# First chunk of an attention and feed-forward kernel: two transfers issued sooner, five additions and the rest of U and V issued later, products with low weight parts issued last

## The chip, the cores and the metric

The kernel runs on one core of a Trainium2 chip. The metric is the device time of one execution in microseconds (us). Engines are named as the profile names them: PE (TensorE matmuls) and PEld (its weight loads), DVE (VectorE), ACT (ScalarE), POOL (GpSimd), and SP, whose queue issues every DMA of this kernel. Each engine works through its own list of instructions in order; they meet only at semaphores.

## The reference

The computation is windowed attention followed by a low-rank token mix and a feed-forward layer, all on float32 inputs:

```python
scores = scale * np.matmul(q, k.transpose(0, 1, 3, 2))     # 8 batches, 8 heads, 576 tokens, 64 wide
mask_plain = (rel >= 0) & (rel < 32)                       # heads 0 to 3
mask_dil = (rel >= 0) & (rel < 128) & (rel % 4 == 0)       # heads 4 to 7
attn = softmax(where(mask, scores, -1e9));  x = (attn @ v), heads side by side: 576 x 512 per batch
h = x.transpose(0, 2, 1) @ U @ V                           # U 576 x 32, V 32 x 576: mixes tokens
u = x + h.transpose(0, 2, 1)
ch = np.maximum(u @ w_ch1, 0.0) @ w_ch2                    # 512 -> 2048 -> 512
return u + ch
```

U, V and the two weights arrive as 64-bit floats, viewed as pairs of 32-bit words.

## The kernel before

**Chunks.** The 36 token tiles of 128 rows are processed by the feed-forward layer in chunks: chunk 0 holds tiles 0 to 3, chunk 1 tiles 4 and 5, every later chunk three tiles. A chunk goes through the 16 slices f of the hidden dimension: `layer1(f)` makes `ph` (12 matmuls of 512 columns in chunk 0), ACT and DVE turn it into a high part `hh` and a low part `hl`, and `layer2(f-1)` adds to one accumulator per tile (4 tiles x 3 matmuls in chunk 0). Each product is made of three, because operands are split into a high and a low part: high x high, high x low weight, low x high weight. In chunk 0 the `ph` buffer of one slice is free again when DVE has made the slice's `hl`, since the fourth accumulator takes one of the two buffers.

**Weights.** All weights are fetched and split during chunk 0. Pieces are numbered in the order of their use: first U (piece 0), V (piece 1), the rest of U and V ("uv", piece 2), then w1 and w2 slices in turn. A piece is fetched into one of four `raw` buffers (`fetch64`, SP), rescaled (`narrow_hi` and `narrow_lo`, lines 199 and 203, ACT), put together (`narrow_b`, lines 207 and 209; 209 runs on DVE for w1 pieces and on POOL for w2 pieces and uv), and split (`narrow_c`: high part of w1 on ACT, line 213, of w2 on DVE, line 215; low part `w1l` or `w2l` on POOL, line 216). Line 209 is the last reader of the raw buffer. `weight_step` runs twice per slice f, moves four pieces one stage on each, and fetches one more: the fetch waits on SP until line 209 of an earlier piece has freed its raw buffer, and everything behind it on SP waits too.

**Attention beside it.** Batch 0's attention (groups 0 to 8, two query blocks of 64 each) is done before chunk 0 in `first_batch`. Batch 1's groups 9 to 17 are spread over chunk 0. Step s of `attention_steps(1)` issues, on SP, v of group 9+s-1 (two DMAs, `load_v`, line 353), k of group 9+s+2 (line 332), and the rows of an earlier group that are scattered into x (`spread_rows`, line 518, five or six DMAs); on PE it issues pv of group 9+s-2 (line 475), the scores s of group 9+s (line 418) and the transposes ptp (line 452); DVE places pv, takes the row minimum and copies the transposed pt (line 458). So v of a group is issued one step ahead of its use. Four v buffers hold two groups.

**The mix of batch 0.** The upper half of the columns of batch 0's x lies in the dilated order of the tokens in `xps`. `leave` writes it to DRAM in eight DMAs (line 823), `come` reads it back in token order in five (line 828). The mixes add h to x: line 595 is one matmul of 256 columns, line 597 the addition by DVE, ten of each. Only the sum u + ch at the end of the chunk and the transposes for chunk 1 (tile 4) read the result; the transposed u that chunk 0 multiplies was made in `first_batch` by `mix_turned`.

**What sets the order.** Inside chunk 0 the order on every engine is the order of the program (`manual_schedule`). Beside the matmuls the program calls `slot()`: two slots inside layer 1, one behind it, three inside layer 2, one behind that, seven for each slice. A list `queue` of pairs (position, work) is taken in order of position; slot number n stands at position 0.01223 n, so one slice f is 0.0856 and chunk 0 ends at 1.33. Batch 1's step s stands at 0.012 + 0.075 s. From chunk 1 on, a planner sets the order of the instructions.

Of the kernel before, what the change touches and what calls it, by code (L numbers as in the profile page):

```python
# [10 lines left out]
F32 = mybir.dt.float32  # L11
F32R = mybir.dt.float32r
# [13 lines left out]
P = 128  # L26
# [105 lines left out]
def batch_parts(b):  # L132
    parts = []
    tok = 0
    while tok < S:
        t, row = divmod(b * S + tok, P)
        n = min(P - row, S - tok)
        parts.append((t, row, n, tok))
        tok += n
    return parts  # L140
# [3 lines left out]
def attention_moe_kernel(ctx: ExitStack, tc: tile.TileContext, qk0, qk2, vv, masks, wide, ident, ut, vt, uv, w1, w2, out):  # L144
# [122 lines left out]
    def narrowed(i):  # L267
        narrow_first(i)
        narrow_second(i)
# [35 lines left out]
    def send(to):  # L305
        while NSMALL + len(sent) < to:
            n = NSMALL + len(sent)
            sent[n] = True
            pipe[n] = fetch64(n)
# [9 lines left out]
    def x_tile(t):  # L319
        if t not in xt:  # L320
            xt[t] = xpool.tile([P, DM], F32, tag="x", name=f"x{t}")
        return xt[t]
# [258 lines left out]
    def t_evict(b, c):  # L581
        r = [slice(i * RANK, (i + 1) * RANK) for i in range(4)]
        tp = t_ps.pop((b, c))
        t_sb[b, c] = ts_ = ts0[c]
        nc.scalar.copy(out=ts_[r[0]], in_=tp[r[0]])
        nc.scalar.copy(out=ts_[r[3]], in_=tp[r[0]])
        nc.vector.tensor_tensor(out=ts_[r[1]], in0=tp[r[0]], in1=ts_[r[0]].bitcast(F32), op=ALU.subtract)

    def mix(b, i, c):
        assert 1 in finished  # L590
        t, row, n, tok = batch_parts(b)[i]
        rs = slice(row, row + n)
        mp = psum.tile([P, HALF_D], F32, tag="ps", name=f"m{b}_{i}_{c}")
        o = 64 + tok - row
        nc.tensor.matmul(mp, lhsT=vs[:, o:o + P], rhs=t_sb[b, c], start=True, stop=True)
        x = x_tile(t)[rs, c * HALF_D:(c + 1) * HALF_D]
        nc.vector.tensor_tensor(out=x, in0=x, in1=mp[rs], op=ALU.add)

    u_ps = {}

# [244 lines left out]
    early_open = ExitStack()  # L845
    early = early_open.enter_context(tc.tile_pool(name="early", bufs=1))
    u32 = early.tile([P, NU * RANK], F32, name="u32")
    ts0 = [early.tile([P, HALF_D], F32R, name=f"ts0_{c}") for c in range(2)]
    q_sb = early.tile([P, NQ, UNITS, 2, QB], F32, name="q_sb")
    idle_sb = early.tile([P, DM], BF16, name="idle_sb")  # L850
    nc.vector.memset(idle_sb, 0.0)
# [2 lines left out]
    for i in range(2):  # L854
        for q1 in q1_sb:
            nc.vector.memset(q1[i * QB:(i + 1) * QB, :, 1 - i], 0.0)
    for t in ts0 + [ts_sb]:
        nc.gpsimd.memset(t[2 * RANK:3 * RANK].bitcast(F32), 0.0)
    for t in pts:
        nc.gpsimd.memset(t, 0.0)  # L860
# [11 lines left out]
    for g in range(1, NGB):  # L872
# [6 lines left out]
        if g == U_AT:  # L879
            pipe[0] = fetch64(0)  # L880
    load_v(NGB - 1, 0)
    for i in range(3, 6):
        send(NSMALL + i)
        if i < 5:
            load_q(NGB + i - 3)
    first_batch()

    held = {}
# [16 lines left out]

    n0 = len(batch_parts(0))
    queue = [(AHEAD_AT[0], lambda: ahead(0)), (AHEAD_AT[1], lambda: ahead(1))]
    queue += [(0.15 + 0.01 * p, lambda p=p: leave(p)) for p in range(NDP)]
    queue += [(0.22 + 0.005 * i, lambda i=i: come(i)) for i in range(n0)]
    queue += [(0.18 + 0.012 * i, lambda i=i: mix(0, i, 0)) for i in range(n0)]  # L910
    queue += [(0.27 + 0.008 * i, lambda i=i: mix(0, i, 1)) for i in range(n0)]

    def fetch_rest():
        pipe[2] = fetch64(2)
# [1 line left out]
    def split_first_u():  # L916
        finish_u(u32[:, 0:4 * RANK], slice(0, 4))
        finish_u(u32[:, 4 * RANK:5 * RANK], slice(8, 9))

    queue += [(0.04, fetch_rest), (0.10, lambda: narrowed(2)), (0.12, lambda: add_low(2, nc.gpsimd)),  # L920
              (0.14, lambda: finish(2)), (0.17, split_first_u)]
    for b in range(1, B):
        lo, hi = (1.5 * b - 2 - LO0, 1.5 * b - 0.5) if b > 2 else (LO2, HI2 + MARGIN)
        its = batch_items(b)
# [11 lines left out]
    for c, tiles in enumerate(CHUNKS):  # L936
        slots = [0]
        nt = len(tiles)
        uh, ul = (e[:, :, 0:nt * P] for e in uts.pop(c))
        acc = [psum.tile([P, DM], F32, tag="acc" if i < CT else "ph", name=f"acc{c}_{i}", bufs=3 if i < CT else 2)  # L940
               for i in range(nt)]
        ht = {}

        def slot():
            pos = (tiles[0] + nt * slots[0] / ((nt + 3) * FC - 3)) / CT
            slots[0] += 1
            while queue and queue[0][0] <= pos:
                queue.pop(0)[1]()

        def layer1(f):  # L950
            assert place_of[f, 0] in finished
            ph = psum.tile([P, CTOK], F32, tag="ph", name=f"ph{c}_{f}", bufs=2)[:, 0:nt * P]
            w1h, w1l = held_w[f][0:2]
            ks = (2, 3, 0, 1) if c == f == 0 else range(KC)
            seq = [(w, u, k) for w, u in ((w1h, uh), (w1l, uh), (w1h, ul)) for k in ks]
            for n, (w, u, k) in enumerate(seq):
                nc.tensor.matmul(ph, lhsT=w[:, k, :], rhs=u[:, k, :], start=(n == 0), stop=(n == len(seq) - 1))  # L957
                if n % KC == KC - 1 and n < len(seq) - 1:
                    slot()
            hh = work.tile([P, CTOK], F32R, tag="hh", name=f"hh{c}_{f}", bufs=2)[:, 0:nt * P]  # L960
            hl = work.tile([P, CTOK], F32R, tag="hl", name=f"hl{c}_{f}", bufs=2)[:, 0:nt * P]
            nc.scalar.activation(out=hh, in_=ph, func=AF.Relu)  # L962
            nc.vector.scalar_tensor_tensor(out=hl, in0=ph, scalar=0.0, in1=hh.bitcast(F32),  # L963
                                           op0=ALU.max, op1=ALU.subtract)
            ht[f] = (hh, hl)

        def layer2(f):
            assert place_of[f, 1] in finished
            hh, hl = ht.pop(f)
            w2h, w2l = held_w[f][2:4]  # L970
            for i in range(nt):
                ss = slice(i * P, (i + 1) * P)
                for n, (h, w) in enumerate(((hh, w2h), (hh, w2l), (hl, w2h))):
                    nc.tensor.matmul(acc[i], lhsT=h[:, ss], rhs=w,  # L974
                                     start=(f == 0 and n == 0), stop=(f == FC - 1 and n == 2))
                if f < FC - 1 and i < nt - 1:
                    slot()

        more = list(CHUNKS[c + 1]) if c + 1 < NCHUNK else []
        for f in range(FC):  # L980
            if c == 0 and f == F_MID - 1:
                after_first()
            if c == 0:
                weight_step()
            layer1(f)
            if f < FC - 1:
                slot()
            else:
                for t in more[0:2]:
                    transp(t)  # L990
            if c == 0:
                weight_step()
            if f > 0:
                layer2(f - 1)
                if f < FC - 1:
                    slot()
        for t in more[2:]:
            transp(t)
        layer2(FC - 1)
        if c == 0:  # L1000
            order.__exit__(None, None, None)
        for i, t in enumerate(tiles):
            x = xt.pop(t)
            nc.vector.tensor_tensor(out=x, in0=acc[i], in1=x, op=ALU.add)  # L1004
            nc.sync.dma_start(out=out[t * P:(t + 1) * P, :], in_=x)
# [87 lines left out]
```

## Time and profile before

| | |
|---|---|
| time, median of 3 runs | 980.51 us (979.42 to 981.93) |
| profiled execution, its own time | 979.55 us |
| its span, first to last instruction | 977.8 us |
| granted TensorE clock, mean | 0.996 |
| busy: PE / DVE / ACT / POOL | 965.0 / 576.5 / 355.9 / 282.8 us |
| chunk 0 (first matmul of layer 1 to the last of layer 2) | 34.9 to 158.9 us of the span |

In a timeline a row gives start, duration, engine, line, operation, the tiles as out<-in, the shapes, the count, and in brackets the idle time before it with what ended it. Engine SPq is SP issuing a DMA; the duration is that of the issue, not of the transfer. In a row of a window the figures are busy us of each engine with the number of instructions, then the granted clock and the share of DMA engines that were busy. Matmul durations overlap: the pace is read from the distance of starts.

### The profile page before, as it was taken

The page shows a single profiled execution, that of the slowest core. Times are in us where ns is not written, and L with a number is a line of the kernel's source. Part 1 is how long each engine was busy: PE and PEld are TensorE (multiplying, and loading weights), DVE is VectorE, ACT ScalarE, POOL GpSimd, SP SyncE. Part 2 cuts the span into 40 slices and gives each one's busy share as a digit, 9 for nine tenths or more (in the row PEclk, how much of TensorE's full clock was granted, in tenths as well). Part 3 has the DMA queues.
Part 4 walks back from the last instruction along what each step waited for, and adds up shares of the span by engine and source line. Part 5 has one row for each costly group of instructions (what it writes and reads, how often), then busy time and mean ns, then how long its engine had stood idle before and what let it go on. Part 6 is the DMA issues. An engine that isn't in the chain of part 4 may idle for free.

```text
span 977.8 us, 17663 instructions
## 1 busy us (share of the span) xinstructions
PE 965.0 (99%) x5906; PEld 835.0 (85%) x5906; DVE 576.5 (59%) x1935; ACT 355.9 (36%) x861; POOL 282.8 (29%) x490
## 2 busy tenths in 40 slices
PE   9989999999999999999999999999999999999998
PEld 7677878988988888888988889888898888999997
DVE  5677777784677747665467746767446864211211
ACT  6755664352344314343244423334233421111110
POOL 4665566252233304241133402343022410000000
PEclk9989999999999999999999999999999999999999
DMA  9477654442344325442233414533323502200000
GB/s 336 142 242 237 196 166 126 132 141 77 89 118 142 97 51 146 125 117 84 76 103 114 130 35 118 148 101 106 89 61 105 158 24 60 81 1 1 33 1 33
DMA packets 100331, 106.14 MB, mean 109 GB/s; under 512 B 12496, under 2 KB 85392, under 8 KB 100240
## 3 DMA queue, kind: packets, MB, share of 16 engines
q1 hardware_dynamic: 100240, 105.01, 36.3%
q8 instruction: 48, 0.79, 0.4%
q14 instruction: 43, 0.35, 0.1%
HBM read 82.94 MB, written 17.89 MB: 103 GB/s over the span
## 4 chain that ended last, share of the span: by engine, by line
PE 89%; DMA 2%; DVE 2%; POOL 2%; issue 2%; SPq 1%; ACT 1%; DVEq 0%; POOLq 0%; ACTq 0%
PE acc L974 38%; PE ph L957 38%; PE pv L475 4%; PE s L405 3%; PE s L418 2%; PE t L555 1%; SPq L518 1%; DMA qkr<-qk 1%; DMA x<-spare 1%; PE ptp L452 1%; PE m L577 1%; POOL v L209 1%; PE idle_ps L867 1%; POOL w1l L216 1%; DVE pt L464 0%
## 5 line engine op out<-in xcount | busy, mean ns | idle before, releaser
L974 PE MATMUL acc<-w2h,hh 128*128 128x512 f32 x576 | 228.4, 397 | 1.1 <-DVE x L1004 0.8
L974 PE MATMUL acc<-w2l,hh 128*128 128x512 f32 x576 | 228.1, 396 | 0.9 <-POOL w2l L216 0.9
L382 POOL TENSOR_TENSOR qks<-qkr,qks 128x160 fp32r<-128x160 f32 x192 | 103.4, 538 | 429.8 <-issue 209.0
L963 DVE SCALAR_TENSOR_TENSOR hl<-ph,hh 128x384 fp32r<-128x384 f32 (+2 forms) x192 | 106.3, 554 | 180.0 <-ACT hh L962 179.1
L974 PE MATMUL acc<-w2h,hl 128*128 128x512 f32 x576 | 212.5, 395 | 0.0
L962 ACT ACTIVATE hh<-ph 128x384 fp32r<-128x384 f32 (+2 forms) x192 | 93.3, 486 | 288.5 <-PE ph L957 279.2
L957 PE MATMUL ph<-utl,w1h 128*128 128x384 f32 (+2 forms) x768 | 171.7, 338 | 0.0
L957 PE MATMUL ph<-uth,w1h 128*128 128x384 f32 (+2 forms) x768 | 170.9, 339 | 0.5 <-DVE hl L963 0.5
L957 PE MATMUL ph<-uth,w1l 128*128 128x384 f32 (+2 forms) x768 | 170.2, 338 | 0.0
L441 ACT ACTIVATE p<-p,nmax 128x160 f32<-128x160 f32 (+1 forms) x288 | 109.3, 406 | 133.4 <-DVE nmax L437 132.2
L957 PEld LDWEIGHTS ph<-uth,w1h 128*128 128x128 f32 x768 | 136.9, 188 | 18.7 <-DVE hl L963 1.4
L464 DVE STREAM_TRANSPOSE pt<-p 32x128 f32<-32x128 f32 x432 | 130.2, 301 | 22.6 <-ACT p L441 17.1
L957 PEld LDWEIGHTS ph<-utl,w1h 128*128 128x128 f32 x768 | 134.2, 188 | 4.5 <-issue 0.8
L957 PEld LDWEIGHTS ph<-uth,w1l 128*128 128x128 f32 x768 | 133.4, 188 | 4.7 <-issue 1.2
L974 PEld LDWEIGHTS acc<-w2h,hl 128*128 128x128 f32 x576 | 108.0, 188 | 23.9 <-issue 1.2
L381 ACT CAST qks<-qkr 128x288 fp32r<-128x288 f32 x192 | 80.8, 430 | 127.9 <-PE s L405 63.4
L974 PEld LDWEIGHTS acc<-w2h,hh 128*128 128x128 f32 x576 | 108.5, 188 | 19.9 <-issue 1.2
L974 PEld LDWEIGHTS acc<-w2l,hh 128*128 128x128 f32 x576 | 108.5, 188 | 17.7 <-POOL w2l L216 1.5
L385 POOL TENSOR_TENSOR qks<-qkr,qks 64x128 fp32r<-64x128 f32 x192 | 90.0, 469 | 15.0
L434 DVE TENSOR_TENSOR p<-s,wide_sb 128x160 f32<-128x160 f32 x192 | 59.3, 319 | 50.2 <-PE s L405 48.1
L437 DVE CUSTOM_DVE_ANT_0 p<-s,p 128x160 f32<-128x160 f32 x192 | 59.7, 320 | 3.5
L475 PEld LDWEIGHTS pv<-v,pt 96*64 96x64 f32 x1152 | 41.1, 138 | 23.5 <-issue 13.0
(90 smaller groups left out, 765.9 us busy)
## 6 DMA issues: line engine op xcount, KB each, us to landing
qkr<-qk SPq DMA_DIRECT2D x192, 144.0 KB, 2.2
v<-vv SPq DMA_DIRECT2D x126, 130.0 KB, 2.4
raw<-w SPq DMA_DIRECT2D x25, 512.0 KB, 4.1
out<-x SPq DMA_DIRECT2D x36, 256.0 KB, 2.4
zd<-z SPq DMA_DIRECT2D x120, 64.0 KB, 2.1
xt<-zd SPq DMA_DIRECT2D x30, 256.0 KB, 2.9
k<-qk SPq DMA_DIRECT2D x18, 320.0 KB, 5.1
raw<-w SPq DMA_DIRECT2D x14, 256.0 KB, 3.4
```

What stands on the lines that cost most here:

```text
L381: nc.scalar.copy(out=t[:, 0:QK2], in_=raw)
L382: nc.gpsimd.tensor_tensor(out=t[:, QK2:], in0=raw[:, P:], in1=t[:, P:QK2].bitcast(F32), op=ALU.subtract)
L385: eng.tensor_tensor(out=t[lo, 0:P], in0=raw[lo, 0:P], in1=t[lo, 0:P].bitcast(F32), op=ALU.subtract)
L434: nc.vector.tensor_tensor(out=p_sb[:, u, :], in0=sp[:, 0:KW], in1=held[0][:, kind], op=ALU.add)
L437: nc.vector.tensor_tensor_reduce(out=p_sb[rs, u, 0:w], in0=a, in1=c, scale=-1.0 / 8.0, scalar=3.0e38, op0=ALU.add, op1=ALU.min, accum_out= ...
L441: nc.scalar.activation(out=p_sb[:, u, 0:w], in_=p_sb[:, u, 0:w], func=AF.Exp, bias=nmax[:, u:u + 1], scale=-1.0,)
L464: nc.vector.transpose(out=pt[WIN * k:WIN * (k + 1), :, rs], in_=p_sb[rs, :, o:o + WIN])
L475: nc.tensor.matmul(pv[rs, u, :], lhsT=pt[:, u, rs], rhs=loaded[g, 1, i][0:KB, u, :], start=True, stop=True)
L957: nc.tensor.matmul(ph, lhsT=w[:, k, :], rhs=u[:, k, :], start=(n == 0), stop=(n == len(seq) - 1))
L962: nc.scalar.activation(out=hh, in_=ph, func=AF.Relu)
L963: nc.vector.scalar_tensor_tensor(out=hl, in0=ph, scalar=0.0, in1=hh.bitcast(F32), op0=ALU.max, op1=ALU.subtract)
L974: nc.tensor.matmul(acc[i], lhsT=h[:, ss], rhs=w, start=(f == 0 and n == 0), stop=(f == FC - 1 and n == 2))
```

## The change

Five things change, all in chunk 0 or ahead of it.

1. v of groups 9 and 10 (four DMAs) is issued ahead of `first_batch`, behind the first two weight pieces and ahead of k of groups 9 and 10; each of these k moves ahead of the weight piece that it followed. Steps 1 and 2 of batch 1 then issue no v.
2. `leave` moves from positions 0.15 to 0.19 to 0.24 to 0.28, `come` from 0.22 to 0.24 to 0.44 to 0.50.
3. The ten mixes of 256 columns at 0.18 to 0.30 become five of 512 columns (`mix_rest`, lines 577 and 579) at 0.60 to 0.72. The evicted U-products go straight into `ts_sb`, so `ts0` and its two memsets go.
4. The fetch of uv moves from 0.04 to 0.30, its stages from 0.10, 0.12 and 0.14 to 0.37, 0.40 and 0.42, and the split of the first part of U from 0.17 to 0.26.
5. In chunk 0 (layer 1 from f = 1) the order of the products is high x high, low x high weight, high x low weight. Layer 2 goes through all four tiles for one product before the next; a slot is called behind each three matmuls as before.

```diff
-        t_sb[b, c] = ts_ = ts0[c]
+        t_sb[b, c] = ts_ = ts_sb[:, c * HALF_D:(c + 1) * HALF_D]
...
-    def mix(b, i, c):
...
     load_v(NGB - 1, 0)
+    send(NSMALL + 2)
+    for g in range(NGB, NGB + 2):
+        for i in range(2):
+            load_v(g, i)
     for i in range(3, 6):
-        send(NSMALL + i)
         if i < 5:
             load_q(NGB + i - 3)
+        send(NSMALL + i)
...
-    queue += [(0.15 + 0.01 * p, lambda p=p: leave(p)) for p in range(NDP)]
-    queue += [(0.22 + 0.005 * i, lambda i=i: come(i)) for i in range(n0)]
-    queue += [(0.18 + 0.012 * i, lambda i=i: mix(0, i, 0)) for i in range(n0)]
-    queue += [(0.27 + 0.008 * i, lambda i=i: mix(0, i, 1)) for i in range(n0)]
+    queue += [(0.24 + 0.01 * p, lambda p=p: leave(p)) for p in range(NDP)]
+    queue += [(0.44 + 0.015 * i, lambda i=i: come(i)) for i in range(n0)]
+    queue += [(0.60 + 0.03 * i, lambda i=i: mix_rest(0, i)) for i in range(n0)]
...
-    queue += [(0.04, fetch_rest), (0.10, lambda: narrowed(2)), (0.12, lambda: add_low(2, nc.gpsimd)),
-              (0.14, lambda: finish(2)), (0.17, split_first_u)]
+    queue += [(0.30, fetch_rest), (0.37, lambda: narrowed(2)), (0.40, lambda: add_low(2, nc.gpsimd)),
+              (0.42, lambda: finish(2)), (0.26, split_first_u)]
...
-            seq = [(w, u, k) for w, u in ((w1h, uh), (w1l, uh), (w1h, ul)) for k in ks]
+            terms = [(w1h, uh), (w1l, uh), (w1h, ul)]
+            if c == 0 and f > 0:
+                terms = [terms[0], terms[2], terms[1]]
+            seq = [(w, u, k) for w, u in terms for k in ks]
...
-            for i in range(nt):
-                ss = slice(i * P, (i + 1) * P)
-                for n, (h, w) in enumerate(((hh, w2h), (hh, w2l), (hl, w2h))):
-                    nc.tensor.matmul(acc[i], lhsT=h[:, ss], rhs=w,
-                                     start=(f == 0 and n == 0), stop=(f == FC - 1 and n == 2))
-                if f < FC - 1 and i < nt - 1:
+            terms = [(hh, w2h), (hh, w2l), (hl, w2h)]
+            seq = [(i, n, term) for i in range(nt) for n, term in enumerate(terms)]
+            if c == 0:
+                terms = [terms[0], terms[2], terms[1]]
+                seq = [(i, n, term) for n, term in enumerate(terms) for i in range(nt)]
+            for m, (i, n, (h, w)) in enumerate(seq):
+                nc.tensor.matmul(acc[i], lhsT=h[:, i * P:(i + 1) * P], rhs=w,
+                                 start=(f == 0 and n == 0), stop=(f == FC - 1 and n == 2))
+                if f < FC - 1 and m % 3 == 2 and m < len(seq) - 1:
                     slot()
```

More of the change, by code (lines that the diff above doesn't have):

```diff
@@ L587, in t_evict @@
         nc.vector.tensor_tensor(out=ts_[r[1]], in0=tp[r[0]], in1=ts_[r[0]].bitcast(F32), op=ALU.subtract)
-    def mix(b, i, c):
[L590 to L597, printed above, removed]
     u_ps = {}
@@ L847, in attention_moe_kernel @@
     u32 = early.tile([P, NU * RANK], F32, name="u32")
-    ts0 = [early.tile([P, HALF_D], F32R, name=f"ts0_{c}") for c in range(2)]
     q_sb = early.tile([P, NQ, UNITS, 2, QB], F32, name="q_sb")
@@ L856, in attention_moe_kernel @@
             nc.vector.memset(q1[i * QB:(i + 1) * QB, :, 1 - i], 0.0)
-    for t in ts0 + [ts_sb]:
+    for t in [ts_sb]:
         nc.gpsimd.memset(t[2 * RANK:3 * RANK].bitcast(F32), 0.0)
```

## The prediction

> **What bounds the kernel now.** I read the page first, then the windows, then PE's timeline in chunk 0, then what its gaps waited for.
>
> ```profile
> PE 965.0 (99%) x5906; PEld 835.0 (85%) x5906; DVE 576.5 (59%) x1935; ACT 355.9 (36%) x861; POOL 282.8 (29%) x490
> PE 89%; DMA 2%; DVE 2%; POOL 2%; issue 2%; SPq 1%; ACT 1%; DVEq 0%; POOLq 0%; ACTq 0%
> ```
>
> PE is busy nearly always and holds most of the chain that ended last: time can be won only where PE stands still or runs slowly. The windows show where.
>
> ```profile
> 50.00:55.00 5.00, 2.55 (x15) 1.71 (x14) 2.69 (x13) 4.04 (x10) 2.85 (x4) 0.98 0.66 222
> 55.00:60.00 5.00, 5.00 (x30) 4.55 (x31) 4.30 (x16) 3.10 (x11) 4.25 (x7) 0.50 0.65 204
> 60.00:65.00 5.00, 5.00 (x23) 4.14 (x22) 2.03 (x5) 2.04 (x6) 2.79 (x3) 0.84 0.84 260
> 81.50:158.90 77.40, 76.86 (x452) 61.03 (x452) 57.81 (x133) 44.09 (x101) 49.33 (x50) 1.00 0.58 184
> 158.90:978.00 819.10, 812.92 (x4902) 715.95 (x4900) 466.92 (x1596) 262.38 (x639) 189.21 (x376) 1.00 0.31 89
> ```
>
> Chunk 0's second half (81.5 to 158.9) leaves 0.5 us of idle PE. What can be won lies between 42 and 81.5, the clock at 0.50 included. These are PE's gaps there, with pv (L475) of groups 9, 10, 11 and 12 as landmarks:
>
> ```profile
> 43.82 0.50 PE L974 MATMUL acc<-w2l,hh 128*128 128x512 f32 x1 [0.89 <-POOL w2l L216]
> 47.77 1.10 PE L957 MATMUL ph<-uth,w1h 128*128 128x512 f32 x4
> 51.69 0.40 PE L974 MATMUL acc<-w2h,hl 128*128 128x512 f32 x1
> 54.27 0.30 PE L475 MATMUL pv<-v,pt 96*64 96x65 f32 x2 [2.18 <-DMA v<-vv]
> 54.83 1.13 PE L475 MATMUL pv<-v,pt 96*64 96x65 f32 x14 [0.27 <-DMA v<-vv]
> 65.49 0.69 PE L475 MATMUL pv<-v,pt 96*64 96x65 f32 x16
> 73.75 0.69 PE L475 MATMUL pv<-v,pt 96*64 96x65 f32 x16
> 76.31 0.61 PE L452 MATMUL ptp<-id_sb,p 128*96 128x128 f32 x4 [0.81 <-DVE x L597]
> 81.45 0.69 PE L475 MATMUL pv<-v,pt 96*64 96x65 f32 x16
> ```
>
> The largest gap is the wait for v of group 9, 2.18 + 0.27 = 2.45 us, and the clock falls behind it: by the windows 5 x (0.02 + 0.50 + 0.16) = 3.4 us of full-speed work are lost. Together 5.8 us. Then 0.89 us for w2l, and 0.81 us at 76.31, where DVE itself stood behind the last `come`.
>
> **The change, part by part.** v of groups 9 and 10 issued early: the stall at 54.27 and the slow clock behind it go, 5.8 us. The four transfers land among the first ones, behind the two weight pieces that `first_batch` needs; what they push back is the first w2 piece, which the layer 2 at 43.82 is the first to use, and k of groups 9 and 10, which now go ahead of weights. So they cost nothing, and the two memsets less win nothing. What is late next is seen in these rows.
>
> ```profile
> 46.61 0.69 DVE L963 SCALAR_TENSOR_TENSOR hl<-ph,hh 128x512 fp32r<-128x512 f32 x1 [1.96 <-ACT hh L962]
> 50.74 0.68 DVE L458 COPY pt<-ptp 96x512 f32<-96x512 f32 x1
> 51.39 0.49 ACT L199 ACTIVATE v<-raw 128x320 f32<-128x320 f32 x1
> 52.17 0.60 ACT L213 CAST w1h<-v 128x512 fp32r<-128x512 f32 x1
> 60.06 0.62 ACT L213 CAST w1h<-v 128x512 fp32r<-128x512 f32 x1
> 60.81 1.29 POOL L216 TENSOR_TENSOR w1l<-v,w1h 128x512 fp32r<-128x512 f32 x1 [0.62 <-POOL q L341]
> 62.61 1.31 POOL L209 TENSOR_TENSOR v<-v,raw 128x512 int32<-128x512 int32 x1 [0.51 <-DVE v L207]
> ```
>
> Low parts last: layer 2 asks for w2l eight matmuls later, and the 0.89 us at 43.82 go (1.14 with the restart). But layer 1 of f = 2, at 47.77, can't start before `hl` is done (46.61 + 0.69 = 47.3), so only some 0.4 us stay; and pv of group 9 needs its pt, done at 50.74 + 0.68 = 51.4. Both are limits of the DVE and ACT chain, which the change doesn't touch before 51. So pv 9 runs at about 51.5, 2.8 us sooner, at full clock.
>
> uv later: at 51.39 ACT does uv's two activations, 52.17 - 51.39 = 0.8 us ahead of w1h. Without them, the chain that ends in POOL's line 209 at 62.61 (piece 15 is fetched into the buffer which that frees) moves up: w1h by 0.8 at 52.17 and at 60.06 alike, w1l to 60.0, and 209 needn't wait for DVE, whose mixes are gone: 61.2 to 62.5. The same work comes back around f = 5, where 76.86 of 77.40 us are PE's; POOL (49.33) and ACT (44.09) have room for 2 us: nothing there.
>
> Now SP's queue, past which `leave` and uv are moved:
>
> ```profile
> 50.55 0.90 SPq L353 DMA_DIRECT2D v<-vv  x2
> 56.64 1.38 SPq L823 DMA_DIRECT2D spare<-xp  x3
> 65.41 0.38 SPq L192 DMA_DIRECT2D raw<-w  x1
> 66.31 0.91 SPq L353 DMA_DIRECT2D v<-vv  x2
> 67.74 0.33 SPq L332 DMA_DIRECT2D k<-qk  x1
> 74.17 0.52 SPq L190 DMA_DIRECT2D raw<-w  x1
> 74.78 0.92 SPq L353 DMA_DIRECT2D v<-vv  x2
> 76.28 3.05 SPq L518 DMA_DIRECT2D x<-xp  x5
> DMA to landing us min/median/max: 3.1/3.9/6.1
> ```
>
> Piece 15 is fetched at 65.41 before. After, its buffer is free at 62.5, and SP, with everything behind it, waits until then. In front of v of group 12 then stand: piece 15, v of 11, k, six scatters of step 3, `leave`'s eight (positions 0.24 to 0.28, between step 3 at 0.237 and step 4 at 0.312), piece 16, and uv (0.30). From the rows: 0.5 + 0.95 + 0.45 + 6 x 0.61 (3.05 / 5) + 8 x 0.46 (1.38 / 3) + 0.5 + 0.4 = 10.1 us, so v 12 is issued at 72.6 to 73.5. v 9 took from 50.55 to PE's 54.27, 3.7 us, behind one weight piece; behind piece 16 and uv it is rather 3.9, the median of the last row (of this line): v 12 is there at 77.0.
>
> PE wants it when? v 11 is issued at 63.0 to 63.9 by the same count and there at some 67.2, where pv 11 runs. From there to pv 12 PE has pv, s, ptp, twelve matmuls of layer 2 and eight of layer 1, here from the chain of waits:
>
> ```profile
> 76.92 2.75 PE acc L974 x12
> 79.67 1.85 PE ph L957 x8
> 81.52 0.62 PE pv L475 x16
> 82.14 1.06 PE s L418 x8
> 83.20 0.44 PE ptp L452 x4
> ```
>
> That is 0.62 + 1.06 + 0.44 + 2.75 + 1.85 = 6.7 us, so PE asks for v 12 at 73.9 and stands until 77.0: **the stall goes from v 9 to v 12** and is 3.1 us long. At this landmark PE is 81.45 - 77.0 = 4.4 us ahead of before, whatever was won earlier: the 0.4 us of the low parts and the 0.81 us at 76.31 lie inside it.
>
> The bounds of this term: 19 issues at the pace of `leave` (0.46) or of the scatters (0.61) take 8.7 to 11.6 us, and a landing takes 3.1 to 6.1 us. v 12 is then there between 74.3, a stall of 0.4 us, and 80.7 (second v half a microsecond behind the first), where only 0.7 us are left of the lead. I take the counts of the rows and the median.
>
> Does the clock fall? The nearest row is the gap of 2.45 us, behind which it was 0.50; 3.1 us is longer, so I take the same loss, 3.4 us, with 0 as the other end. [...]
>
> What is still due behind pv 12:
>
> ```profile
> L579 DVE TENSOR_TENSOR x<-x,m x5: 646/675/691, 133.8 to 147.2; 128x512 f32<-128x512 f32 x4, 64x512 f32<-64x512 f32 x1
> 110.00:120.00 10.00, 10.00 (x64) 7.96 (x60) 8.62 (x17) 4.72 (x9) 5.95 (x6) 1.00 0.72 225
> 156.99 2.79 DVE L1004 TENSOR_TENSOR x<-acc,x 128x512 f32<-128x512 f32 x4 [0.25 <-PE acc L974]
> ```
>
> The ten mixes lay ahead of 81.45 before; the five lie behind it now: five matmuls of 512 columns, 2.75 / 12 = 0.23 each, 1.15 us. DVE has their additions, 5 x 0.675 = 3.4 us, near a stretch in which it is busy 8.62 of 10: between 0 and 3.4, and I take 0.5, since they are spread over 1.4 slices (0.60 to 0.72), more than 10 us, and even the full stretch has 1.4 of 10 us free. `come`'s five reads now stand in front of v 14 and v 15: 0 to 1, I take 0.3. At the end of the chunk the first accumulator was done nine matmuls before the last; now all four end with the last four, so DVE's additions (2.79 us, begun at 156.99) begin 6 x 0.23 = 1.4 us later. The fourth accumulator gives `ph` its second buffer back, which chunk 1's second slice wants at once: 0 to 1.4, I take 0.7. Below nothing none of these can be: they add or delay work. The rest of the kernel (812.92 of 819.10 us PE) passes a lead or a lag on.
>
> The sum against the profiled execution: -4.4 + 1.15 + 3.4 + 0.5 + 0.3 + 0.7 = +1.65, so 979.55 + 1.65 = 981.2 us. That execution lay 0.96 us under the median of 980.51; I put nothing on top for it.
>
> **The rivals.**
>
> *The stall comes back but the clock stays.* 981.2 - 3.4 = 977.8 us. For it: behind the gap of 0.81 us at 76.31 the window from 81.5 has 1.00, so the bound lies somewhere between, and nothing says that the same gap always counts alike. Against it: 2.45 us sufficed.
>
> *v 12 is in time.* If SP is quicker (the bound of 74.3 with little else), PE passes pv 12 at 73.9, a lead of 7.55: 979.55 - 7.55 + 1.15 + 0.5 + 0.3 + 0.7 = 974.7 us. For it: SP's rows hold waits that may go with `come`. Against it: piece 15's buffer is tied to POOL and nothing of the change makes that earlier than 62.
>
> *Slower: a second stall.* `come` (0.44 to 0.50) and the scatters of steps 5 and 6 stand in front of v 14, as `leave` did in front of v 12. If v 14 lands over 2.2 us behind PE's wish, PE stands 2.45 us and the clock falls again: +5.8, 987.0 us; it decides from where SP is more than one step behind PE. For it: five reads of DRAM more in that step, of 128 KB each. Against it: with a half clock behind pv 12 PE gives SP 3.4 us to catch up, and SP issued v 12 at 74.78, 6.7 us ahead of its use.
>
> **How the numbers follow.** Chances: the forecast 0.45 (its own range 979 to 984), clock stays 0.2, v 12 in time 0.2, second stall 0.15. About 0.3%, 2.9 us, is what a measurement of this kernel can tell from no change: faster is below 977.6, slower above 983.4. Faster holds the third case and somewhat under half of the second, 0.28; slower the fourth and the top of the first, 0.22; the rest is 0.50. The range goes from 974.0, where v 12 is in time with the unknown costs near nothing, to 985.0, which leaves out most of the second stall.
>
> **What would show it.** Right: no wait at pv 9, which runs near 51.5; no w2l wait; a wait of pv for v some 25 us later, near 74 to 77, with SP's eight `leave` rows right ahead of the v; a window with clock 0.50 behind it; no wait of ptp for line 597's successor. Wrong: pv 12 without a wait, or piece 15's fetch well before 62, and then the gain of about 5 us stays; waits of `ph` for `hl` around the five additions would make DVE's term larger, and a gap at the first two slices of chunk 1 would give the chunk end's.

## The result and the profile after

The changed kernel takes **985.91 us** (median of 6 runs, 984.65 to 987.25) against 980.53 us of the kernel before on the same chip: ratio **1.0057, 95% interval 1.0043 to 1.0071**, 5.4 us slower. The prediction was 981.2 with a range up to 985.0. Its profiled execution took 984.65 us (span 982.9), 5.10 more than that of before, so the two traces hold nearly the whole difference. Medians below are over all executions, ratios leave out the few with a lowered clock, so the two can differ a little.

First the page of the kernel after, the busy times:

```profile
PE 967.3 (98%) x5901; PEld 834.7 (85%) x5901; DVE 576.1 (59%) x1930; ACT 357.5 (36%) x861; POOL 282.8 (29%) x488
```

PE is 2.3 us longer busy, with the same work in five instructions fewer (five mixes in place of ten). The windows of the kernel after (busy us by engine, then clock, DMA share, GB/s) and PE's waits in chunk 0 (total, times, longest):

```profile
50.00:55.00 5.00, 5.00 (x42) 4.10 (x41) 2.72 (x13) 4.45 (x10) 3.42 (x4) 1.00 0.58 205
...
75.00:80.00 5.00, 1.53 (x17) 1.34 (x18) 0.42 (x2) 2.60 (x5) 2.86 (x3) 0.88 0.86 299
80.00:85.00 5.00, 5.00 (x24) 4.48 (x25) 2.93 (x14) 2.71 (x7) 0.44 (x2) 0.77 0.95 324
110.00:120.00 10.00, 9.27 (x68) 7.19 (x69) 8.99 (x18) 3.65 (x7) 5.41 (x4) 1.00 0.72 229
```

```profile
PE pv L475 <- DMA v<-vv: 4.2, 1, 4.2
...
PE m L577 <- DVE x L505: 0.7, 1, 0.7
PE ph L952 <- DVE hl L958: 0.6, 1, 0.6
PE ptp L452 <- DVE ssum L481: 0.2, 1, 0.2
```

The stall went from v of group 9 to v of group 12. These are PE's landmarks of the kernel after: slice 2's first matmul, pv of groups 9, 12, 13 and 14, and the start of chunk 1, which was at 158.90 before.

```profile
47.49 1.18 PE L952 MATMUL ph<-uth,w1h 128*128 128x512 f32 x4 [0.61 <-DVE hl L958]
...
51.83 0.69 PE L475 MATMUL pv<-v,pt 96*64 96x65 f32 x16
...
78.47 1.33 PE L475 MATMUL pv<-v,pt 96*64 96x65 f32 x16 [4.19 <-DMA v<-vv]
...
87.09 0.69 PE L475 MATMUL pv<-v,pt 96*64 96x65 f32 x16
...
93.89 0.92 PE L475 MATMUL pv<-v,pt 96*64 96x65 f32 x16
...
159.82 0.64 PE L952 MATMUL ph<-uth,w1h 128*128 128x256 f32 x4
```

So **chunk 0 ends only 0.92 us later** than before. The rest of the loss comes where the diff changes nothing. The last three matmuls of the kernel before and of the kernel after:

```profile
972.21 0.86 PE L974 MATMUL acc<-w2h,hl 128*128 128x512 f32 x3
```

```profile
977.30 0.86 PE L972 MATMUL acc<-w2h,hl 128*128 128x512 f32 x3
```

The lag has grown to 5.09 us: 4.17 us arise between 159 and 977. Is it waiting? One window over the steady part, before, then after:

```profile
230.00:900.00 670.00, 668.75 (x4020) 586.35 (x4019) 397.77 (x1354) 220.10 (x534) 159.85 (x318) 1.00 0.33 92
```

```profile
230.00:900.00 670.00, 668.51 (x4006) 584.10 (x4005) 397.82 (x1354) 220.45 (x533) 159.93 (x318) 1.00 0.32 92
```

Hardly: PE is busy as long, at full clock. It gets 14 matmuls less done in 670 us, which alone proves little: matmuls of several lengths fall into the window, and kernels below whose tiles lie as before have 4004 to 4020 in it. The pace says more. One slice in the middle of both traces shows which matmuls take longer: nine matmuls of layer 2, then the next slice's layer 1.

```profile
563.67 0.39 PE L974 MATMUL acc<-w2h,hh 128*128 128x512 f32 x1
...
565.73 0.86 PE L957 MATMUL ph<-uth,w1h 128*128 128x384 f32 x4
566.43 0.85 PE L957 MATMUL ph<-uth,w1l 128*128 128x384 f32 x4
```

```profile
566.70 0.40 PE L972 MATMUL acc<-w2h,hh 128*128 128x512 f32 x1
...
568.79 0.86 PE L952 MATMUL ph<-uth,w1h 128*128 128x384 f32 x4
569.49 0.86 PE L952 MATMUL ph<-uth,w1l 128*128 128x384 f32 x4
```

Nine layer-2 matmuls take 2.06 us before and 2.09 us after; four of layer 1 take 0.70 in both. Over the whole trace (distance of starts, chunks 2 to 11, mean) the product hh x w2h goes from 229.5 to 233.8 ns in slices 0 to 12 and layer 1 stays at 173.5. The two other products of layer 2 lose 1.7 and 3.7 ns, so 3.2 in the mean; 1536 matmuls of layer 2 lie behind chunk 0, 13/16 of them in these slices, and 1248 x 3.2 ns = 4.0 us. Layer 1 of slices 13 to 15 runs 1.3 ns faster, 396 matmuls, and takes 0.5 us back. The other 0.5 us are idle PE, 1.8 us in place of 1.25 behind chunk 0.

The last chunk shows the loss by itself, since PE has nothing but the two layers there, and no wait. From its first row to the row of the last three matmuls it takes 972.21 - 904.37 = 67.84 us before and 977.30 - 908.95 = 68.35 us after:

```profile
904.37 0.87 PE L957 MATMUL ph<-uth,w1h 128*128 128x384 f32 x4
```

```profile
908.95 0.86 PE L952 MATMUL ph<-uth,w1h 128*128 128x384 f32 x4
```

What differs for these matmuls? Not their order or their shapes, but where their operands lie. In these programs a pool gives a tile its place in SBUF when its tag is first used. With v of group 9 issued ahead of the first batch, the tag of v (4 tiles of 1056 B) comes ahead of those of k, p, ssum, nmax, hh and hl, which used to come before it, and these lie 4224 B higher in the compiled program: hh at 51008 and 53056 B in place of 46784 and 48832.

### The profile page after: what moved, and what is told of

Same layout as the page of the kernel before. It is cut to its first block, busy times and chain, and to the rows that moved or that the text cites. A ratio compares the mean times of both kernels' runs of the same rounds, so it can differ in the third digit from the quotient of the medians.

```text
span 982.9 us, 17647 instructions
## 1 busy us (share of the span) xinstructions
PE 967.3 (98%) x5901; PEld 834.7 (85%) x5901; DVE 576.1 (59%) x1930; ACT 357.5 (36%) x861; POOL 282.8 (29%) x488
## 4 chain that ended last, share of the span: by engine, by line
PE 89%; DVE 3%; ACT 2%; issue 2%; POOL 2%; DMA 1%; SPq 1%; DVEq 0%; POOLq 0%; ACTq 0%
PE acc L972 38%; PE ph L952 38%; PE pv L475 4%; PE s L405 3%; PE t L555 2%; PE s L418 2%; DVE v L209 1%; PE m L577 1%; ACT p L441 1%; SPq L518 1%; POOL v L209 1%; PE idle_ps L856 1%; POOL w1l L216 1%; PE ptp L452 0%; DMA qkr<-qk 0%
## 5 line engine op out<-in xcount | busy, mean ns | idle before, releaser
L972 PE MATMUL acc<-w2h,hh 128*128 128x512 f32 x576 | 221.5, 397 | 1.6 <-DVE x L1002 1.0
L972 PE MATMUL acc<-w2l,hh 128*128 128x512 f32 x576 | 221.1, 396 | 0.0
L972 PE MATMUL acc<-w2h,hl 128*128 128x512 f32 x576 | 206.0, 397 | 0.0
```

The lines of the kernel that those rows point to most:

```text
L972: nc.tensor.matmul(acc[i], lhsT=h[:, i * P:(i + 1) * P], rhs=w, start=(f == 0 and n == 0), stop=(f == FC - 1 and n == 2))
```

## Experiments on the address

**Only the shift.** The kernel before, with v's tag created first.

```diff
+    work.tile([P, UNITS, VW], F32, tag="v", name="first_v", bufs=4)
     idle(9)
     load_q(0)
```

> The kernel before with one difference: the v tag is created ahead of the others, so that qks, p, hh and hl lie 4224 bytes higher, as in the changed kernel; no instruction changes. Theory A (addresses): layer 2 at 232.5 ns, 984.5 to 985 us, slower than before by 4 us, chunk 0 as before with v of group 9 late. Theory B (order): 980.5, no difference.

Measured: 983.81 us against 980.38, ratio 1.0035 (1.0024 to 1.0045), with no instruction changed: the addresses alone cost 3.4 us. In its trace hh x w2h has the pace of the changed kernel, 233.8 ns, and the last chunk takes 68.4 us. Of the 4.26 us between its profiled execution and that of before, 3.1 arise behind chunk 0; the other 1.15 us arise in chunk 0, where one wait, of ptp for DVE, is 1.6 us longer than in that execution of before.

**The shift undone.** The kernel after, with the tags created in the order of before.

```diff
+    for tag, shape, n in (("qks", ...), ("p", ...), ("ssum", ...), ("nmax", ...), ("hh", ...), ("hl", ...)):
+        work.tile(shape, ..., tag=tag, name=f"first_{tag}", bufs=n)
     idle(9)
     load_q(0)
```

> The changed kernel with one difference: the pools' tags in SBUF are created in the order of before, so that hh, hl, p, qks and v lie at their old addresses; every instruction is the changed kernel's. Theory A (the 4 us that are lost between chunk 1 and the end come from where hh and hl lie in SBUF, since the matmuls of layer 2 run 232.5 ns apart instead of 229.6): layer 2 back at 229.6 ns in later chunks, time 982, that is 4 us under the changed kernel, chunk 0 as in it. Theory B (the lost time comes from the order or the waits that chunk 0 hands on): layer 2 stays at 232.5 ns and the time at 986.

Measured: 983.09 us, ratio 1.0019 (1.0011 to 1.0028). 3.8 of the 5.7 thousandths go; the change without its side effect costs 1.9 us. The pace at the old addresses is read from the next kernel, whose later chunks have the same instructions: hh x w2h 229.6 ns.

**Early v left out.** The kernel after, with v of groups 9 and 10 issued by their steps again; the addresses are then those of before by themselves.

```diff
     send(NSMALL + 2)
-    for g in range(NGB, NGB + 2):
-        for i in range(2):
-            load_v(g, i)
```

> The changed kernel without its first part: v of groups 9 and 10 is issued in steps 1 and 2 as before (addresses are then those of before by themselves). Theory SP (what costs in chunk 0 is the order of SP's queue): the fetch ahead of v 9 no longer waits behind uv, so v 9 is there about 52 to 53 and PE waits 0.5 to 1 us there; v of group 12 is as late as in the changed kernel, about 4 us. Chunk 0 ends within 1.5 us of the changed kernel's, and with theory A on the addresses the time is 981 to 983; with theory B 985 to 987.

Measured: 981.97 us, ratio 1.0017 (1.0008 to 1.0026), the same as with early v at the old addresses. PE's rows of pv 9 and pv 12:

```profile
52.18 0.68 PE L475 MATMUL pv<-v,pt 96*64 96x65 f32 x14 [0.41 <-DMA v<-vv]
...
77.93 1.40 PE L475 MATMUL pv<-v,pt 96*64 96x65 f32 x16 [4.03 <-DMA v<-vv]
```

The stall at pv 9 is 0.41 us in place of 2.45, though v 9 is issued by its step: SP issues it at 47.72 in place of 50.55, where the fetch of uv (47.63) and the next piece stood ahead of it. So the other parts of the change, the later uv most likely, took away most of what the prediction gave to early v. The 4 us are again those of pv 12, which comes when the queue allows, whatever the small lead at v 9.

**128 B in place of 4224.** The kernel before, with hh, hl and v moved by 128 B and all behind them by 512.

```diff
+    for tag, shape, n in (..., ("nmax", [P, UNITS], 2), ("gap", [P, 32], 1), ("hh", ...), ("hl", ...),
+                          ("v", [P, UNITS, VW], 4), ("gap2", [P, 96], 1)):
+        work.tile(shape, ..., tag=tag, name=f"first_{tag}", bufs=n)
     idle(9)
     load_q(0)
```

> The kernel before with no instruction changed: one gap of 128 B is put into the work pool ahead of hh, and one of 384 B behind v. So hh, hl and v lie 128 B higher (hh at 46912 and 48960 in place of 46784 and 48832), the tiles ahead of them (k, p, ssum, nmax) stay, and all that lies behind them, the w2 tiles among them, moves by 512 B. Theory A (what slowed layer 2 in the changed kernel is where hh and hl lie within 512 B, as against w2; 4224 B is 128 more than 8 times 512): layer-2 matmuls again take about 3 ns more in f 0 to 12 (229.6 to about 232.5 ns), and the time is 3 to 4.5 us longer, ratio 1.003 to 1.0045. Rival B (the place of hh and hl as a whole counts, or that of k, p and v that moved along): within 1 us of the kernel before.

Measured: 983.52 us against 980.19, ratio 1.004 (1.0027 to 1.0053), as slow as 4224 B. k, p, ssum and nmax, which didn't move, are out as a cause, and so is a large distance. v did move, but the last chunk, which doesn't use it, is as slow as with 4224 B (68.4 us).

**The last weight pool.** Slices 13 to 15 were slower already in the kernel before (232.5 ns in layer 2, 176.4 in layer 1); their weights lie at another residue within 512 B, 480 in place of 192.

```diff
         t2 = [pool.tile([P, n, DM], F32R, name=f"w2{i}_{lo}") for i in "hl"]
+        if lo == F_LAST:
+            pool.tile([P, 72], F32, name="w_gap")
```

> The kernel before with no instruction changed: a gap of 288 B in the last weight pool (f 13 to 15), so that its w1 and w2 tiles lie 288 B lower (w2h at 216768 in place of 217056) and have the residue of 192 within 512 B that those of f 0 to 12 have. Theory A (the residues of hh, hl, u and the weights against each other set the pace): layer 2 of f 13 to 15 falls from 232.7 to about 229.6 ns, layer 1 from 176.4 to about 173.5 ns; 3 f times 11 chunks times 9 matmuls times 3 ns (0.9 us) and 3 times 11 times 12 times 2.9 ns (1.15 us), so about 2 us less, ratio 0.9975 to 0.9985. Rival B (f 13 to 15 are slow for another cause, the end of the chunk's work around them): the paces stay and the time is within 0.5 us.

Measured: **977.24 us, ratio 0.997 (0.9957 to 0.9983)**, by one gap of 288 B and no other edit. That is 2.9 us where 2 were forecast. The traces with a granted clock of 0.996 to 0.999 bear out some 2: from the start of chunk 1 to that of the last matmul the five kernels here with this gap take 812.0 to 812.6 us, the five with hh and the weights where they lay before 813.4 to 815.8 (the kernel before itself 813.8), and the three with hh moved 816.7 to 818.0. The last chunk, measured as above, takes 67.5 us in all of the first group, 67.8 in all of the second and 68.4 in all of the third, whatever chunk 0 was like.

The paces (ns from start to start, means over chunks 2 to 11 of each trace; residue of the address within 512 B in brackets):

| | before | after | hh by 128 B | last pool moved |
|---|---|---|---|---|
| hh x w2h, slices 0 to 12 | 229.5 (192, 192) | 233.8 (320, 192) | 234.1 (320, 192) | 229.4 (192, 192) |
| hh x w2l, slices 0 to 12 | 229.8 | 231.5 | 231.3 | 229.8 |
| hh x w2h, slices 13 to 15 | 232.5 (192, 480) | 233.4 (320, 480) | 233.5 (320, 480) | 229.5 (192, 192) |
| layer 1, slices 0 to 12 | 173.5 | 173.6 | 173.5 | 173.5 |
| layer 1, slices 13 to 15 | 176.4 | 175.1 | 174.9 | 173.5 |

So in these runs the pace of both layers went with where tiles lie (229.4 to 234.1 ns for hh x w2h, 173.5 to 176.4 ns for layer 1). The residue within 512 B is one way of listing it: 4224 and 128 B, which cost the same, differ by 4096 B, so a period that divides 4096 would fit, and no run tells which. "Equal residues" isn't the rule: in layer 1 of slices 0 to 12 u lies at residue 0 and w1 at 192, and that is fast (173.5 ns).

An obvious rival is a clash with the other engines, since ACT and DVE write hh and hl at the moved addresses too. The traces speak against it: among the matmuls of hh x w2h (slices 0 to 12, chunks 2 to 11) during which DVE, ACT, POOL and all DMA stand idle, 38 in each trace, the mean pace goes from 227.8 ns before to 236.4 ns after, a larger step than over all of them. So it is there without any of them at work; what makes it, no run tells. Nor is it a matter of a matmul's own two operands alone: layer 1 of slices 13 to 15 went from 176.4 to 175.1 ns, and neither u nor w1 had moved.

## Experiments on chunk 0

**`leave` early.** The kernel after at the old addresses, `leave` back at 0.15 to 0.19.

```diff
-    queue += [(0.24 + 0.01 * p, lambda p=p: leave(p)) for p in range(NDP)]
+    queue += [(0.15 + 0.01 * p, lambda p=p: leave(p)) for p in range(NDP)]
```

> The changed kernel with the addresses of before, and leave back at positions 0.15 to 0.19. Theory SP: eight issues of 0.46 us fewer ahead of v 12, which comes 3.5 us sooner; its wait falls from 4.2 to under 1.5 us and the clock stays at full; chunk 0 ends 2 to 4 us sooner than in the run with the addresses alone, 977 to 980 us in all with theory A. Rival (the wait is handed to v 13 and v 14, as SP issues the same work): chunk 0 ends as late, 981 to 983.

Measured: 981.01 us, ratio 1.0009 (0.9999 to 1.0019).

```profile
PE pv L475 <- DMA v<-vv: 3.6, 4, 1.5
```

One wait of 4.2 us became four of 1.5 at most: without the eight issues of `leave` v 12 is issued at 71.84 in place of 73.93 and nearly in time, and v 13 and v 14 are late behind the row transfers of the step before and weight fetches. That the clock would stay was wrong: it falls behind the last of these waits, 1.46 us at 92.62, and 5 x (0.11 + 0.23) = 1.7 us are lost. The kernel is at par with before.

```profile
90.00:95.00 5.00, 3.54 (x31) 2.87 (x30) 3.62 (x8) 0.53 (x1) 2.11 (x3) 0.89 0.70 230
95.00:100.00 5.00, 5.00 (x21) 4.17 (x20) 1.82 (x10) 3.33 (x9) 2.56 (x2) 0.77 0.85 254
```

**v a step sooner.** The same, and each step asks for its own group's v right behind the products that free the buffers, ahead of the row transfers.

```diff
-                if 0 < s <= NGB:
+                if b >= SPLIT and 0 < s <= NGB:
                     load_v(g - 1, 0)
                     load_v(g - 1, 1)
                 if b < SPLIT and s + 2 < NGB:
                     load_q(g + 2)
+                if s >= LAG:
+                    weighted(g - LAG, held.pop(g - LAG))
+                if b < SPLIT and s < NGB:
+                    load_v(g, 0)
+                    load_v(g, 1)
                 if b < SPLIT and g - LAG - 1 in scatter:
                     spread_rows(g - LAG - 1)
-                if s >= LAG:
-                    weighted(g - LAG, held.pop(g - LAG))
```

> The changed kernel with hh, hl and the rest at the addresses of before, the spare copies of the mixes' right halves back at 0.15 to 0.19, and batch 1's v asked for one step sooner: in each step the loads of v for the group of that step stand right behind the products that free their buffers, ahead of the six to eight row transfers, instead of at the head of the next step. Theory (v12 to v14 come late only because their loads wait behind SyncE's row transfers; those waits were 3.6 us together in the kernel without this edit): the four waits on v fall to under 0.5 us together, chunk 0 ends 2 to 3 us sooner than there, time 978 to 979.5, ratio 0.998 to 0.9995. Rival (the transfers queue up, and what is freed at v returns as waits on the row transfers, the mixes or the products' inputs): 980.5 to 981.5.

Measured: 979.35 us, ratio 0.9991 (0.9978 to 1.0003).

```profile
PE ph L958 <- DVE hl L964: 2.7, 3, 1.7
PE ptp L452 <- DVE ssum L481: 2.1, 1, 2.1
```

No wait for v is left, and chunk 0 ends 2.5 us sooner than in the kernel before this one (chunk 1 starts at 157.30 in place of 159.77): both as forecast, and the time lies in the forecast range. Against the kernel before the change the interval holds 1, so a gain isn't clear of noise. Part of what was freed went where the rival sent it, into waits for DVE: hl, and ssum, behind which a PSUM buffer comes free; behind that wait of 2.1 us the clock falls and 1.7 us are lost (the mean granted clock of this execution is 0.998).

**Both.** The kernel with v a step sooner, and the gap in the last pool.

```diff
+        if lo == F_LAST:
+            pool.tile([P, 72], F32, name="w_gap")
```

> The same as the one with v a step sooner, and the last weight pool 288 B lower. Both theories right: the two gains add up, 976 to 977.5, ratio 0.9955 to 0.9975. Only the addresses right: 978.3 to 979.3. Only v right: 978 to 979.5. Neither: 980.5 to 981.5.

Measured: 977.37 us, ratio 0.9976 (0.9966 to 0.9985): no further than the gap in the last pool alone, and 2 us under the kernel without the gap. Its largest wait in chunk 0, in PE's timeline and then DVE's:

```profile
99.89 0.85 PE L454 MATMUL ptp<-id_sb,p 128*96 128x128 f32 x4 [2.79 <-DVE ssum L483]
```

```profile
97.51 1.64 DVE L211 CUSTOM_DVE_ANT_0 v<-raw,v 128x1024 uint16<-128x1024 uint16 x1
99.07 0.67 DVE L581 TENSOR_TENSOR x<-x,m 128x512 f32<-128x512 f32 x1
```

In this trace the deferred mixes are in the way: m takes one of three PSUM buffers, its addition waits behind a weight's recombination on DVE, and the step's ptp waits for the next buffer.

**Mixes behind the steps.** On top of both:

```diff
-    queue += [(0.60 + 0.03 * i, lambda i=i: mix_rest(0, i)) for i in range(n0)]
+    queue += [(0.80 + 0.035 * i, lambda i=i: mix_rest(0, i)) for i in range(n0)]
```

> The kernel with v a step sooner and the last weight pool 288 B lower, and the five mixes at 0.80 to 0.94 in place of 0.60 to 0.72, behind the last step of batch 1. In that kernel PE stood 2.79 us before ptp at 99.89, since the first mix's PSUM buffer is freed by DVE's addition at 99.07, behind a weight's recombination of 1.65 us, and the clock fell to 0.66 in 100 to 105. Theory (the mixes take a PSUM buffer and DVE out of the steps' chain): that wait falls under 0.5 us and the clock stays, 2.3 to 4.5 us less, 973 to 975.2, ratio against the kernel before 0.9925 to 0.995. Rival (the weights' chain on DVE, ACT and POOL sets the pace from 95 on, and the lead goes into waits for hl or pt): 976.5 to 977.8.

In this kernel and the next the last two mixes stand behind the sum of batch 1's product with U (0.90), which goes into the tile that they read: they add batch 1's product in place of batch 0's, the amount of work is unchanged, but what these two kernels return is not what the reference does. Measured: 977.37 us, ratio 0.9974 (0.9963 to 0.9985).

```profile
PE ph L960 <- DVE hl L966: 3.1, 2, 2.5
PE m L579 <- DVE ts_sb L570: 2.2, 1, 2.2
```

The wait for ssum went as expected, the gain didn't come: the time is the rival's. One wait is that of m for batch 1's sum, which the crossing makes. The longer wait for hl, 2.47 us at 82.27, lies ahead of both places of the mixes, so the move didn't make it; the clock fell behind it, to 0.73 in 80 to 85 and 0.59 in 85 to 90, and 5 x (0.27 + 0.41) = 3.4 us were lost.

**The product order of before.** On top of that:

```diff
-            if c == 0 and f > 0:
-                terms = [terms[0], terms[2], terms[1]]
...
-            if c == 0:
-                terms = [terms[0], terms[2], terms[1]]
-                seq = [(i, n, term) for n, term in enumerate(terms) for i in range(nt)]
```

> The same with the fifth part of the change undone: in chunk 0 the products stand in the order of before (weights' low parts second in layer 1, tile by tile in layer 2). Theory (low parts last is worth what the prediction took, some 0.4 us at the second slice, and costs up to 1.4 us at the end of the chunk where all four accumulators end together): within 1 us of the kernel with low parts last, more likely shorter by 0 to 0.7. Rival (the low parts of the weights are what comes latest in the whole of chunk 0, on POOL): waits for w1l and w2l appear, 1 to 4 us longer.

Measured: 977.99 us, ratio 0.9978 (0.9967 to 0.9988), no difference that can be told.

```profile
PE m L579 <- DVE ts_sb L570: 3.1, 1, 3.1
PE ph L958 <- DVE hl L964: 1.8, 2, 0.9
PE acc L975 <- POOL w2l L218: 0.9, 1, 0.9
```

The wait of 0.9 us for w2l is back, as before the change, and in these two traces those for hl are 1.3 us shorter. That low parts last exchanges one for the other fits this; two traces don't show it.

**Early v alone.** The first part of the change, on the kernel before and its addresses.

```diff
+    for tag, shape, n in (("qks", ...), ...):
+        work.tile(shape, ..., tag=tag, name=f"first_{tag}", bufs=n)
...
+    send(NSMALL + 2)
+    for g in range(NGB, NGB + 2):
+        for i in range(2):
+            load_v(g, i)
     for i in range(3, 6):
-        send(NSMALL + i)
         if i < 5:
             load_q(NGB + i - 3)
+        send(NSMALL + i)
```

> The kernel before with the first part of the change alone, v of groups 9 and 10 issued ahead of the first batch's work, all tiles at the addresses of before. The wait of 2.45 us for v 9 goes, and with it the half clock behind. Theory (nothing moves v 12: before it was issued at 74.8 and there at about 78.5, and PE asks for it some 5.8 us sooner, at 75.6): a wait of 2 to 3.5 us at pv 12, with or without 1.7 us of lost clock, so 977.5 to 980, ratio 0.997 to 0.9995. Rival 1 (the rest passes the lead on): 974 to 976. Rival 2 (the later steps eat all of it): 980 to 981.5.

Measured: **978.65 us, ratio 0.9981 (0.9971 to 0.9991)**, within the theory's numbers, but by another wait. pv 9 has none (51.31), and then:

```profile
57.92 0.55 PE L595 MATMUL m<-ts,vs 128*128 128x256 f32 x1 [3.73 <-DVE xp L505]
```

```profile
55.00:60.00 5.00, 2.08 (x6) 1.82 (x7) 4.30 (x16) 3.80 (x13) 3.74 (x6) 0.67 0.77 259
60.00:65.00 5.00, 5.00 (x17) 4.02 (x17) 2.52 (x4) 1.44 (x3) 2.57 (x2) 0.65 0.83 268
```

The early mix asks for a PSUM buffer that DVE has not freed, 3.7 us, and the clock falls, 5 x (0.33 + 0.35) = 3.4 us. The kernel before has the wait for v 9 and not this one (with hh moved by 128 B it has both, this one 1.4 us); the changed kernel, with the mixes moved, has no wait of over 0.6 us between 50 and 65.

**Mixes between the steps and batch 1's sum.** v a step sooner, the gap in the last pool, the product order of before, and the mixes at 0.775 to 0.847.

```diff
-    queue += [(0.80 + 0.035 * i, lambda i=i: mix_rest(0, i)) for i in range(n0)]
+    queue += [(0.775 + 0.018 * i, lambda i=i: mix_rest(0, i)) for i in range(n0)]
```

> The kernel with v a step sooner, the last weight pool 288 B lower and the product order of before, the five mixes now at 0.775 to 0.847: behind the last step of batch 1 (0.762) and ahead of batch 1's own product with U (0.86), whose sum goes into the tile that the mixes read. With the mixes at 0.80 to 0.94 the last two stood behind that sum: PE waited 3.11 us for it at 125.45, while up to slice 11 it had been 4.6 us ahead of the kernel before. Theory (that wait was made by the crossing alone): it goes, chunk 0 ends 3.5 to 5 us ahead of before, and with some 2.1 us from the addresses the time is 973.5 to 975.5, ratio 0.9935 to 0.9955. Rival (from 112 on DVE sets the pace: five additions in 8 us now lie beside the weights' steps, and the lead goes into waits for hl or w2l): 976.5 to 977.8, ratio 0.9965 to 0.9978.

Measured: **974.25 us against 979.92, ratio 0.9949 (0.9934 to 0.9964)**, 5.7 us under the kernel before and, by 0.9949 / 1.0057, 1.1% under the changed one. Its waits in chunk 0, and the start of chunk 1:

```profile
PE ph L958 <- DVE hl L964: 2.3, 2, 2.1
PE m L579 <- DVE x L507: 1.0, 1, 1.0
...
PE acc L975 <- POOL w2l L218: 0.9, 1, 0.9
```

```profile
154.99 0.64 PE L958 MATMUL ph<-uth,w1h 128*128 128x256 f32 x4
```

Chunk 0 ends 3.9 us ahead of before (158.90); the rest of the 5.5 us between the two profiled executions (979.55 and 974.06) arises behind it, where only the addresses of the last pool differ. The wait for the sum is gone, and so is the fall of the clock behind it: the crossing was what had held the mixes back.

## Why the prediction was wrong

- **The failed step: "The rest of the kernel (812.92 of 819.10 us PE) passes a lead or a lag on."** It passes it on and adds 4.17 us of its own, some 3.6 of them by the slower pace. That PE is full there was read right; that its pace stays was assumed. Undoing the shift takes 3.7 us off the result, making the shift alone puts 3.4 us on the kernel before. "So they cost nothing", said of the early transfers, left this out: an earlier first use of a tag moves other tiles. Why the pace follows the addresses stays open. What remains, 1.9 us by the ratio of the kernel at the old addresses, is near the predicted 1.65, and partly by luck: against the trace, the sum had the lead 1.4 us too large, the clock's loss 1.65 us too large and the rest of chunk 0 some 0.5 us too large, and these nearly cancel.
- **The base, a smaller miss.** The sum starts from the profiled execution of before and puts nothing on top for the 0.96 us to the median; by medians the same sum gives 980.51 + 1.65 = 982.2 us. The changed kernel's median, too, lies 1.26 us above its profiled execution.
- **pv 9, right.** Forecast "at about 51.5", found at 51.83 with no wait and a clock of 1.00 in 50 to 55. But it wasn't early v that took most of the stall away: with the other parts of the change alone, v 9 issued by its step costs 0.41 us. And it is worth nothing by itself behind a late `leave`: without early v the time is the same.
- **"The stall goes from v 9 to v 12", right, and mis-sized.** PE asked at 78.47 - 4.19 = 74.3 (forecast 73.9); v was there at 78.5 (forecast 77.0). SP's rows of the kernel after show the count that was forecast, piece 15 first and uv last:

```profile
62.66 0.33 SPq L192 DMA_DIRECT2D raw<-w  x1
63.04 0.90 SPq L353 DMA_DIRECT2D v<-vv  x2
...
64.51 3.75 SPq L518 DMA_DIRECT2D x<-xp  x6
68.31 4.33 SPq L813 DMA_DIRECT2D spare<-xp  x8
...
73.38 0.46 SPq L192 DMA_DIRECT2D raw<-uv  x1
73.93 0.86 SPq L353 DMA_DIRECT2D v<-vv  x2
```

  `leave` took 4.33 / 8 = 0.54 us an issue in place of 0.46, and from the issue at 73.93 to PE's start went 4.5 us in place of 3.9. The issues that the prediction counted for its bounds are 20 and not 19, which moves either bound by some half a microsecond. The lead at this landmark is 81.45 - 78.47 = 3.0 us, not 4.4.
- **The clock, mis-sized the other way.** 5 x (0.12 + 0.23) = 1.75 us were lost behind the 4.19 us, where 3.4 was taken from the gap of 2.45 us.
- **Mixes, additions, `come` and chunk end**, forecast 1.15 + 0.5 + 0.3 + 0.7 = 2.65 us between pv 12 and chunk 1. From -3.0 + 1.75 to +0.92 it is 2.2 us. The 1.15 us of matmuls are an estimate from the pace of before; 0.7 + 0.2 of waits for m and ptp come with them (the window 110 to 120 shows 0.73 idle). `come` cost nothing: pv 13 and 14 don't wait. The accumulators did end together, with no wait of PE for them:

```profile
159.32 2.48 DVE L1002 TENSOR_TENSOR x<-acc,x 128x512 f32<-128x512 f32 x4 [1.42 <-PE acc L972]
```

- **Low parts last, right as to its limit.** The w2l wait is gone, slice 2 starts at 47.49, 0.28 us sooner (forecast 0.4), and hl holds it.
- **The rivals.** v 12 wasn't in time; the clock fell and cost half of what was taken. No second stall for v came. The slower side that decided was none of the four: the address.

## What to carry to other kernels

Where later chunks slow down evenly with PE busy and no wait, compare the time of each chunk first, and then where the matmuls' operands lie: an edit that first uses a tile's tag elsewhere moves the tiles of other tags (here by 4224 B), and two extra lines that create the tags in the old order tell this apart from the edit itself. On SP's queue a transfer made early was worth what the next one on that queue allowed (at the old addresses the ratio is 1.0019 with early v and 1.0017 without); the larger gain in chunk 0 came only in the kernel in which v of every step stands ahead of the row transfers and the mixes have left the steps' PSUM buffers.

## What the runs showed of the hardware

**In these runs the pace of a matmul changed with where tiles lie in SBUF.** 128 B more for hh made a layer-2 matmul some 1.5 to 4.6 ns (0.7 to 2%) slower; 288 B less for three slices' weights made it 3 ns faster in those slices. The slowdown was there with DVE, ACT, POOL and DMA idle too (227.8 ns before, 236.4 after), and idle PE makes up little of it: over 230 to 900 PE is busy 668.75 us of 670 before and 668.51 after. What the addresses act on was not shown.

**In these traces a fall of the clock cost some 1.7 or 3.4 us, and the gap's length says neither which nor whether it falls.** From the windows behind each gap: after 1.46 us 1.7 (`leave` early), after 2.45 us 3.4 (before), after 2.79 us 1.7 (v a step sooner with the gap in the last pool), after 3.73 us 3.4 (early v alone), after 4.19 us 1.75 (after), and nothing after 2.06 us (the last kernel) and 2.20 us (mixes behind the steps). The rows for 2.79 and 2.06 us:

```profile
100.00:105.00 5.00, 5.00 (x18) 4.04 (x18) 3.30 (x14) 2.84 (x7) 1.93 (x2) 0.66 0.71 244
```

```profile
81.28 1.20 PE L958 MATMUL ph<-uth,w1h 128*128 128x512 f32 x4 [2.06 <-DVE hl L964]
```

```profile
80.00:85.00 5.00, 3.73 (x35) 3.12 (x36) 4.40 (x8) 3.21 (x9) 3.23 (x4) 1.00 0.70 231
```

What decides between 0, 1.7 and 3.4 us, no run here shows. A bound on the gap alone does not fit: behind 1.46 us the clock fell, behind 2.06 and 2.20 us it stayed at 1.00.
